# Stacking phi beside P in the attention stage of an attention + two-MoE kernel

## The chip, the cores and the metric

The kernel runs on one core of a Trainium2 chip. The metric is the device time of one execution in microseconds, taken over several runs; a profile of one execution gives the trace.

## The reference

Three layers follow each other. The first is attention with a memory, for B = 4 batches, H = 8 heads, S = 576 tokens and D = 64; its output, transposed to 2304 tokens of 512 numbers, goes through two feed-forward layers of 512 -> 2048 -> 512 with weights in 64 bits, the first with mish, the second with silu.

```python
scores = scale * q @ k.T                       # causal, then softmax
local  = softmax(scores) @ v
phi    = lambda x: np.where(x > 0, x, np.exp(x) - 1) + 1
mem    = (phi(q) @ M_prev) / (phi(q) @ z_prev + 1e-6)
g      = sigmoid(beta)
attn   = g * mem + (1 - g) * local
h = attn @ w_in;  out1 = (h * tanh(softplus(h))) @ w_out     # layer 1
h = out1 @ w_in2; out  = silu(h) @ w_out2                    # layer 2
```

phi(q) is also exp(min(q, 0)) + max(q, 0).

## The kernel before

The attention stage works on 16 pairs of heads (two heads of one batch at a time, head 0 in partitions 0 to 63 and head 1 in 64 to 127 where that matters). Every step of a pair is a named operation: `pair_steps` gives its engine, an assumed duration and what it needs, `Attn.steps` what it issues. A planner (`Steps.plan`) lists all operations of the program in order of a latest time plus an offset for its kind (`SHIFT`), and that order is the order in which each engine's queue runs; nothing at run time waits for the planner's times. Engines: P = TensorE, D = VectorE (DVE), A = ScalarE (ACT), G = GpSimd (POOL), S = the DMA queue of SyncE.

For each pair:

- Loads: `ldkT`, `ldqT`, `ldnq` (q by tokens), `ldnv`.
- Scores: TensorE makes q k for query blocks 4, 3, 2, 1 (128 queries each) and 0 (64 queries) in PSUM ring `s` (L561, L597); DVE adds the mask and takes the row minimum in one pass (`r..`, L554); ACT takes the exponential into tiles P4 to P0 and sums rows into `z` (`e..`, L578).
- phi: `phe` = exp(q) and `phu` = q + 1 on ACT (L502, L503), `phf` = max(min(e, 1), u) on DVE (L504), `phz` = phi times z_prev on POOL (L506), `phr` the row sum on DVE (L508), `phg`, `phd` small DVE steps (L509, L512), `phq` multiplies by the row sums (L513), `phm` scales phi by that on POOL (L515). Each of them works on 640 columns, of which a half of the first 128 is zero padding.
- Row sums: `za` on DVE (L604) and `zd`, the reciprocal (L606); POOL makes `zg` (the factors, L607) and `n00` (block 0 scaled, L610).
- Transpositions: TensorE turns P, phi (`T`), the factors (`RT`) and block 0 (`Xs`) by 64x64 blocks into PSUM ring `t` (L483). The copies out of PSUM go to `W0` (phi under or over P's first 64 keys) and to `h1`, `h2`, `h3` (the other keys), by ACT (`hi`, L473) and DVE (`vec`, L476). phi and P's first keys come from different transpositions, so each copy into `W0` fills 64 partitions.
- Values: `Vhi`, `Vlo` multiply with v and M_prev on TensorE (L667); `Vhic`, `Vloc` (DVE, L671) and `Vlo0` (ACT) write the result to `xT`.

Beside this the weights of the first MoE group are decoded from 64 bits during attention: eight jobs, each with four DVE steps (L787, L789, L791, L794), and some steps of them on POOL (L820, L839). After attention, `open0` and `open1` hand PSUM and SBUF to the MoE part; its products (L973 to L975) and second matmuls (L1041) fill TensorE until the end.

Of the kernel before, what the change touches and what calls it, by code (L numbers as in the profile page):

```python
# [202 lines left out]
P = 128  # L203
B, H, S, D = 4, 8, 576, 64
# [19 lines left out]
def dve(n):  # L224
# [7 lines left out]
}  # L232
AB = "AB"
# [23 lines left out]
def pair_steps():  # L257
# [4 lines left out]
    E("phe", "A", act(640, False), ["ldnq"])  # L262
    E("phu", "A", act(640, False), ["ldnq"])
    E("phf", "D", dve(640), ["phe", "phu"])
    E("phz", "G", 1.57, ["phf"])
    E("phr", "D", dve(640), ["phz"])
    E("phg", "D", 0.09, ["phr"])
    E("phd", "D", 0.13, ["phg"], 0.1)
    qk = ["ldkT", "ldqT"]
    for i in (4, 3, 2, 1):  # L270
# [17 lines left out]
        if i == 1:  # L288
            m.group("s", ("s0", "P", 0.25, qk), [("r00", "D", dve(ST), ["s0"], 0.17)])
            E("e00", "A", act(ST, False, 2), ["r00"])  # L290
            m.uses.append(("sm", "r00", ["r00"], ["e00"]))
            exps = ["e00"] + [f"e{x}{y}" for x in range(1, 5) for y in range(2)]
            E("za", "D", 0.15, exps)
            E("zd", "D", 0.15, ["za"], 0.1)
            E("zg", "G", 1.2, ["zd"])
# [37 lines left out]
class Attn:  # L333
# [12 lines left out]
        "W0": ([P, 2, S], F32, ["T", "X1", "X3", "Xs"], VA, 2),
        "P4": ([P, 2, S], F32, ["e40", "e41"], ["X1", "X2"], 2),
        "P3": ([P, 2, width(3)], F32, ["e30", "e31"], ["X1", "X2"], 2),
        "P2": ([P, 2, width(2)], F32, ["e20", "e21"], ["X3"], 2),
        "P1": ([P, 2, width(1)], F32, ["e10", "e11"], ["X3"], 2),  # L350
        "P0": ([P, 2, ST], F32, ["e00"], ["Xs"], 2),
# [5 lines left out]
    TILES["z"] = ([P, 10], F32, ["e00", "e10", "e11", "e20", "e21", "e30", "e31", "e40", "e41"], ["zd", "phq"], 2)  # L357
    TILES["r"] = ([P, 10], F32, ["zd"], ["zg", "n00"], 2)
    TILES["rx"] = ([P, 4, 2, D], F32, ["zg"], ["RT"], 2)
    TILES["R"] = ([P, S - ST], F32, ["RT"], ["Vhic", "Vloc"], 2)  # L360
    for _g in GROUPS:
        TILES[f"h{_g}"] = ([P, 8 if _g == 2 else 6, P], F32, [f"X{_g}"], ["Vlo" if _g == 3 else "Vhi"], 2)
# [20 lines left out]
    def get(self, p, nm):  # L383
        s = self.st[p]
        if nm not in s:
            shape, dt, _, _, cap = self.TILES[nm]
            if nm == "nq":
                s[nm] = self.kept[nm][p % 2]
            else:
                s[nm] = self.pool(nm).tile(shape, dt, tag=nm, name=nm, bufs=cap)  # L390
# [10 lines left out]
    def consts(self):  # L401
        nc, cp, ep = self.nc, self.wp["late"], self.wp["early"]
        self.kept = {"nq": []}
# [17 lines left out]
        for nm, w in (("bt0", H), ("g", H), ("g1", H), ("g1s", NP), ("bt5", 5 * H)):  # L421
            setattr(self, nm, cp.tile([P, w], F32, name=nm))
        for n in range(2):
            t = self.pool("nq").tile([P, 5, 2, D], F32, name=f"nq{n}")
            nc.gpsimd.memset(t[:ST, 0], 0.0)
            self.kept["nq"].append(t)
        self.load(0, "kT", nc.scalar)

    def gates(self):
# [9 lines left out]
        def sig():  # L439
# [4 lines left out]
            b5 = self.bt5.rearrange("p (c h) -> p c h", c=5)  # L444
            for j in range(2):
# [3 lines left out]
            nc.vector.tensor_copy(b5[:, 0, :], bt)  # L449
            nc.vector.tensor_tensor(  # L450
                b5[:, 1:, :], self.g1.unsqueeze(1).to_broadcast([P, 4, H]), bt.unsqueeze(1).to_broadcast([P, 4, H]), op=ALU.mult)
        return ld, exp, sig

    def load(self, p, nm, queue=None):
# [4 lines left out]
        if nm == "nq":  # L459
            queue.dma_start(t[:, 1:].rearrange("p c j d -> p (c j d)"), src[:, 2 * D:])  # L460
            queue.dma_start(t[ST:, 0].rearrange("p j d -> p (j d)"), src[ST:, :2 * D])
        else:
            queue.dma_start(t.rearrange("p c j d -> p (c j d)") if nm == "nv" else t, src)
        bt = self.bt[b]
        if hp == 0 and nm == "nq":
# [3 lines left out]
                self.z[b].rearrange("h d -> (h d)").unsqueeze(0).to_broadcast([P, H * D]))  # L469

# [14 lines left out]
    def kcols(self, j, w):  # L485
        return slice(S + ST - w, S + ST) if j else slice(0, w)

    def mcols(self, j, w):
        return self.mask[:, S - P:S - P + w] if j else self.mask[:, S - w:S]

    def steps(self, p):
# [6 lines left out]
        for nm in ("kT", "qT", "nq", "nv"):  # L498
# [14 lines left out]
        f["phq"] = lambda: nc.vector.tensor_tensor(  # L513
            s["c"][:, 1:], s["c"][:, 1:], s["z"][:, 2:].rearrange("p (c j) -> p c j", j=2), op=ALU.mult)
        f["phm"] = lambda: nc.gpsimd.tensor_tensor(  # L515
            s["e"], s["e"], s["c"].unsqueeze(3).to_broadcast([P, 5, 2, D]), op=ALU.mult)

        def T():
            s["TA"], s["TB"] = self.psum("t"), self.psum("t")
            e = s["e"].rearrange("p c j d -> p c (j d)")  # L520
            self.halves((s["TA"], s["TB"]), [(e[R[0], c] if c else None, e[R[1], c]) for c in range(5)])
        f["T"] = T

        def Th(a):
            for j in range(2):
                w = G("W0")[R[j], j, :]
                ps = s["T" + a].rearrange("p (c x) -> p c x", x=ST)[R[j]]
                if a == "A":
                    self.hi(w[:, ST:].rearrange("p (c x) -> p c x", x=P)[:, :, :ST], ps[:, 1:5])
                else:  # L530
                    self.hi(w.rearrange("p (c x) -> p c x", x=ST)[:, ::2], ps[:, :5])
# [68 lines left out]
        def r00():  # L600
# [4 lines left out]
            s["z"][:, 1:], s["z"][:, 1:], 1.0, 1e-9, op0=ALU.mult, op1=ALU.add)  # L605
        f["zd"] = lambda: nc.vector.reciprocal(G("r")[:, 1:], s["z"][:, 1:])  # L606
        f["zg"] = lambda: nc.gpsimd.tensor_tensor(  # L607
            G("rx"), s["r"][:, 2:].rearrange("p (c j) -> p c j", j=2).unsqueeze(3).to_broadcast([P, 4, 2, D]),
            self.g1[:, h0:h0 + 2].unsqueeze(1).unsqueeze(3).to_broadcast([P, 4, 2, D]), op=ALU.mult)
        f["n00"] = lambda: nc.gpsimd.tensor_scalar(  # L610
            s["P0"], s["P0"][:, 1].unsqueeze(1).to_broadcast([P, 2, ST]), s["r"][:, 1:2],
            self.g1s[:, hp:hp + 1], op0=ALU.mult, op1=ALU.mult)

        def X(g):
# [3 lines left out]
            for key, chunks in GROUPS[g]:  # L618
# [801 lines left out]
```

## Time and profile before

| | us |
|---|---|
| median of 3 runs (lowest, highest) | 989.54 (987.35, 991.29) |
| the profiled execution, its time | 987.81 |
| its span, first to last instruction | 985.2 |
| mean granted TensorE clock, share of full | 0.994 |
| busy: TensorE 938.0, DVE 698.3, ACT 532.0, POOL 94.1 | |

The profile's rows are of the profiled execution; its time is 2.6 us above its span, and 1.73 us below the median. The page cuts the span into 40 slices of 24.6 us; attention fills the first nine.

### The profile page before, as it was taken

What the parts mean: (1) busy time and instruction counts of PE and PEld (TensorE: products, weight loads), DVE (VectorE), ACT (ScalarE), POOL (GpSimd) and SP (SyncE); (2) the same over time, 40 slices, a digit from 0 to 9 for tenths busy, and PEclk for the clock granted to TensorE, in tenths of its full rate; (3) what the DMA queues carried; (4) which work ended last, traced back from release to release, by engine and by line L of the source; (5) the groups of instructions that cost most, each with busy time, mean ns of one, the idle gap of its engine ahead of it and who ended that gap; (6) DMA issues with size and microseconds to landing.
All of it is one profiled execution on the core that took longest, in us unless ns stands there. A gap on an engine that the chain in (4) does not pass through costs nothing.

```text
span 985.2 us, 17546 instructions
## 1 busy us (share of the span) xinstructions
PE 938.0 (95%) x6672; PEld 823.0 (84%) x6672; DVE 698.3 (71%) x1635; ACT 532.0 (54%) x1263; POOL 94.1 (10%) x97
## 2 busy tenths in 40 slices
PE   5888888889999999999999999999999999999998
PEld 3555555568999999989999998898898988898986
DVE  6899999999569665774767699947654955564333
ACT  6899999878555424343343465745443433434330
POOL 3346454430000000000000000000000000000000
PEclk9899999999999999999999999999999999999999
DMA  6444444146646640364055453741570356024412
GB/s 209 120 124 135 124 134 124 50 154 249 248 144 178 234 161 1 116 226 165 24 191 212 186 234 119 261 129 44 195 249 22 94 192 208 15 72 160 149 54 96
DMA packets 56323, 142.95 MB, mean 145 GB/s; under 512 B 5040, under 2 KB 23472, under 8 KB 56240
## 3 DMA queue, kind: packets, MB, share of 16 engines
q1 hardware_dynamic: 56096, 141.52, 42.3%
q8 instruction: 52, 0.85, 0.4%
q10 hardware_dynamic: 144, 0.33, 0.1%
q14 instruction: 31, 0.25, 0.1%
HBM read 104.08 MB, written 37.75 MB: 144 GB/s over the span
## 4 chain that ended last, share of the span: by engine, by line
PE 80%; DVE 11%; ACT 6%; issue 2%; DMA 1%; POOL 0%; SPq 0%; DVEq 0%; POOLq 0%; ACTq 0%
PE acc L1041 41%; PE psX L973 7%; PE psX L974 7%; PE psX L975 7%; PE psY L974 3%; PE psY L973 3%; PE psY L975 3%; DVE sm L554 3%; ACT P L578 3%; PE ps_s L561 2%; PE psW L973 2%; PE psW L974 2%; PE psW L975 2%; DVE h L476 1%; ACT W L473 1%
## 5 line engine op out<-in xcount | busy, mean ns | idle before, releaser
L1041 PE MATMUL acc<-g,w 128*128 128x320 f32 (+1 forms) x1152 | 218.1, 337 | 0.0
L1041 PE MATMUL acc<-w,g 128*128 128x512 f32 x864 | 216.5, 394 | 0.0
L1041 PEld LDWEIGHTS acc<-g,w 128*128 128x128 f32 x1152 | 183.9, 188 | 13.2
L1041 PEld LDWEIGHTS acc<-w,g 128*128 128x128 f32 x864 | 157.1, 188 | 29.4
L1004 ACT COPY vt<-psX 128x256 f32<-128x256 f32 (+1 forms) x192 | 75.9, 398 | 181.3 <-PE psX L975 177.6
L1062 DVE TENSOR_TENSOR xT<-acc,xT 128x512 f32<-128x512 f32 (+1 forms) x126 | 77.1, 613 | 78.1 <-PE acc L1041 77.1
L1014 DVE TENSOR_TENSOR g<-vt,g 128x640 fp32r<-128x640 f32 (+1 forms) x128 | 94.5, 753 | 43.8 <-ACT g L1013 43.3
L1002 DVE TENSOR_TENSOR vt<-psY,vt 128x256 f32<-128x256 f32 (+1 forms) x128 | 57.6, 455 | 78.2 <-PE psY L975 45.8
L1013 ACT CAST g<-vt 128x640 fp32r<-128x640 f32 (+1 forms) x128 | 83.0, 672 | 29.7 <-PE acc L1041 28.6
L578 ACT ACTIVATE P<-sm,m 128x448 f32<-128x448 f32 (+4 forms) x144 | 83.2, 579 | 6.9 <-DVE m L554 6.3
L561 PE MATMUL ps_s<-kT,qT 64*128 64x288 f32 (+3 forms) x320 | 70.3, 479 | 9.6 <-DMA qT<-in_qT_dram 7.9
L973 PE MATMUL psX<-x,w 128*128 128x256 f32 (+1 forms) x256 | 75.7, 296 | 0.0
L974 PE MATMUL psX<-x,w 128*128 128x256 f32 (+1 forms) x256 | 75.6, 295 | 0.0
L975 PE MATMUL psX<-x,w 128*128 128x256 f32 (+1 forms) x256 | 75.6, 295 | 0.0
L1002 DVE TENSOR_TENSOR vt<-psW,vt 128x256 f32<-128x256 f32 (+1 forms) x64 | 29.1, 455 | 50.9 <-PE psW L975 50.8
L1010 ACT ACTIVATE vt<-vt 128x640 f32<-128x640 f32 (+1 forms) x64 | 43.7, 685 | 39.4 <-DVE vt L1002 39.4
L483 PEld LDWEIGHTS ps_t<-ident,P 64*128 64x128 f32 x800 | 35.3, 140 | 34.4 <-DVE xT L671 11.3
L483 PE MATMUL ps_t<-ident,P 64*128 64x64 f32 x800 | 45.4, 231 | 15.9 <-DVE xT L671 6.8
L1008 ACT ACTIVATE vt<-vt 128x256 f32<-128x256 f32 (+1 forms) x64 | 28.5, 446 | 56.3 <-DVE vt L1002 56.2
L554 DVE CUSTOM_DVE_ANT_0 sm<-ps_s,mask 128x288 f32<-128x288 f32 (+3 forms) x128 | 57.1, 467 | 1.2 <-ACT P L578 0.7
L1009 ACT ACTIVATE vt<-psX 128x256 f32<-128x256 f32 (+1 forms) x64 | 26.1, 409 | 49.7 <-PE psX L975 49.4
L973 PEld LDWEIGHTS psX<-x,w 128*128 128x128 f32 x256 | 48.2, 188 | 2.5 <-issue 0.2
(114 smaller groups left out, 2020.2 us busy)
## 6 DMA issues: line engine op xcount, KB each, us to landing
stg<-in_moe_w_in_dram SPq DMA_DIRECT2D x32, 512.0 KB, 5.5
stg<-in_moe_w_out_dram SPq DMA_DIRECT2D x32, 512.0 KB, 4.1
x<-sp SPq DMA_DIRECT2D x18, 640.0 KB, 5.5
x<-sp SPq DMA_DIRECT2D x18, 512.0 KB, 4.7
sp<-x SPq DMA_DIRECT2D x12, 640.0 KB, 3.7
sp<-x SPq DMA_DIRECT2D x12, 512.0 KB, 3.9
nv<-in_v_dram SPq DMA_DIRECT2D x16, 320.0 KB, 3.5
x1T<-sp01T SPq DMA_DIRECT2D x8, 640.0 KB, 5.0
```

The lines of the kernel that those rows point to most:

```text
L483: self.nc.tensor.transpose(to[:, n * ST:(n + 1) * ST], src[x], self.ident[r, r])
L554: nc.vector.tensor_tensor_reduce(out, ps, mask, -0.125, init, ALU.add, ALU.min, acc)
L561: nc.tensor.matmul(ps, lhsT=s["qT"][R[j], qcols(i)], rhs=s["kT"][R[j], k0 + cols.start:k0 + cols.stop], start=True, stop=True)
L578: nc.scalar.activation(G(f"P{i}")[:, 1 - j if i else 1], s[f"sm{i}{j}"], AF.Exp, bias=s[f"m{i}"][:, j:j + 1], scale=-1.0, accum_out=G("z") ...
L973: nc.tensor.matmul(o, lhsT=W(0, kc), rhs=X(0, kc), start=(n in (1, 2, 7) and kc == 0), stop=False, skip_group_check=True)
L974: nc.tensor.matmul(o, lhsT=W(0, kc), rhs=X(1, kc), start=False, stop=False, skip_group_check=True)
L975: nc.tensor.matmul(o, lhsT=W(1, kc), rhs=X(0, kc), start=False, stop=(kc == 1), skip_group_check=True)
L1002: nc.vector.tensor_tensor(o, self.bank[q, to], o, op=ALU.add)
L1013: f[f"h{c}"] = lambda c=c: nc.scalar.copy(hi(c), val(c))
L1014: f[f"l{c}"] = lambda c=c: nc.vector.tensor_tensor(self.gt(q, c)[:, 1, :2 * tb], val(c), hi(c).bitcast(F32), op=ALU.subtract)
L1041: nc.tensor.matmul(y, lhsT=a, rhs=b, start=(c == 0 and k == 0), stop=(c == 1 and k == 5))
L1062: nc.vector.tensor_tensor(part, acc, part, op=ALU.add)
```

## The change

phi no longer has its own transposition. For query blocks 1 to 4, P is written as `[P of head 0 | phi of both heads | P of head 1]` in one row (tiles `Ph` for blocks 3 and 4, `Pl` for 1 and 2; keys of one head now run backwards so that its first 64 keys lie next to phi). A 128-column slice then holds P's first 64 keys and phi side by side, and one transposition (`W`, 16 of them) stacks both over 128 partitions. Block 0 does the same inside `X3`. So `T`, `Xs` and the copies of 64 partitions are gone: each copy out of PSUM has 128 partitions. The copies are shared out by the list `ON_ACT`; the others are on DVE.

phi is exp(min(q, 0)) + max(q, 0) over 576 columns (no padding): `phn` and `phu` (min, max), `phf` (the sum), `phz` and `phy` (times z_prev) on POOL, `phe` (the exponential) alone on ACT. `phm` becomes `phmh`, `phml`, `phm0` on POOL, which write into the P tiles. One DMA loads q instead of two; z_prev gets two more small loads for each batch. The factors' tile `rx` moves to the pool that `open0` waits for, and so `open0` now waits for `zg` and `RT` instead of `T`. The whole `SHIFT` table has new values; `PERIOD` stays.

```diff
-    E("phe", "A", act(640, False), ["ldnq"])
-    E("phu", "A", act(640, False), ["ldnq"])
-    E("phf", "D", dve(640), ["phe", "phu"])
-    E("phz", "G", 1.57, ["phf"])
-    E("phr", "D", dve(640), ["phz"])
+    E("phn", "G", 0.75, ["ldnq"])
+    E("phe", "A", 0.58, ["phn"])
+    E("phu", "G", 0.75, ["ldnq"])
+    E("phf", "G", 1.25, ["phe", "phu"])
+    E("phz", "G", 1.25, ["phf"])
+    E("phy", "G", 0.36, ["phf"])
+    E("phr", "D", dve(576), ["phz", "phy"])
...
+ON_ACT = ("WA", "X1A", "X2A", "X2B", "X3A")
...
+    def evict(n, d, deps, w, more=0.0):
+        m.twin("t", (n, "P", d, deps), [
+            [(f"{n}{a}h", "A", act(w) + more, [n]) if n + a in ON_ACT else (f"{n}{a}h", "D", dve(w) + more, [n])] for a in AB])
...
-            E("phm", "G", 1.28, ["phq"])
+            E("phmh", "G", 0.75, ["phq"])
+            E("phml", "G", 0.75, ["phq"])
+            E("phm0", "G", 0.36, ["phd"])
...
-            m.twin("t", ("T", "P", 0.45, ["phm"]), [[("TAh", "A", 0.58, ["T"])], [("TBh", "A", 0.69, ["T"])]])
+            evict("W", 0.52, ["phmh", "phml"] + exps[1:], 512)
...
-            for g in (1, 2):
-                X(g, hi)
+            evict("X1", 0.52, hi, 512)
+            evict("X2", 0.42, hi, 384)
...
-            X(3, lo)
-            m.twin("t", ("Xs", "P", 0.12, ["n00"]), [[("XsAh", "D", 0.23, ["Xs"])], [("XsBh", "D", 0.23, ["Xs"])]])
+            evict("X3", 0.48, lo + ["n00", "phm0"], 384, 0.14)
...
-        f["phe"] = lambda: nc.scalar.activation(self.get(p, "e"), s["nq"], AF.Exp)
-        f["phu"] = lambda: nc.scalar.activation(self.get(p, "u"), s["nq"], AF.Identity, bias=1.0)
-        f["phf"] = lambda: nc.vector.scalar_tensor_tensor(
-            out=s["e"], in0=s["e"], scalar=1.0, in1=s["u"], op0=ALU.min, op1=ALU.max)
+        f["phn"] = lambda: nc.gpsimd.tensor_scalar(self.get(p, "e"), s["nq"], 0.0, None, op0=ALU.min)
+        f["phe"] = lambda: nc.scalar.activation(s["e"], s["e"], AF.Exp)
+        f["phu"] = lambda: nc.gpsimd.tensor_scalar(self.get(p, "u"), s["nq"], 0.0, None, op0=ALU.max)
+        f["phf"] = lambda: nc.gpsimd.tensor_tensor(s["e"], s["e"], s["u"], op=ALU.add)
...
+        f["phy"] = lambda: nc.gpsimd.tensor_tensor(s["u"][:, 8], s["e"][:, 8], self.bt[b]["y"][:, hp], op=ALU.mult)
...
+        def Wh(a):
+            x = AB.index(a)
+            put("W", a)(G("W0")[:, :, ST:].rearrange("p j (c x) -> p j c x", x=P)[:, :, :, x * ST:(x + 1) * ST],
+                        s["W"][x].rearrange("p (j c x) -> p j c x", j=2, x=ST))
...
+            bt["y"] = self.wp["early"].tile([P, NP, D], F32, tag="y", name="y", bufs=2)
+            for j in range(2):
+                queue.dma_start(
...
-        early = [n for n in self.pair.ops if n[:2] in ("ld", "ph") or n[0] in "Tsre"]
+        early = [n for n in self.pair.ops if n[:2] in ("ld", "ph", "zg", "RT") and n[-1] != "h" or n[:2] == "ph" or n[0] in "sre"]
```

## Rows read from the trace of the kernel before

**Rows 1.** The page, the span in 40 slices (busy tenths of each).
```profile
PE   5888888889999999999999999999999999999998
DVE  6899999999569665774767699947654955564333
```

**Rows 2.** Stretches, us: busy PE, PEld, DVE, ACT, POOL (counts), clock, DMA share, GB/s.
```profile
19.94:204.32 184.38, 155.31 (x1751) 103.28 (x1753) 176.07 (x613) 171.59 (x516) 82.55 (x77) 0.97 0.38 115
...
204.32:228.00 23.68, 20.06 (x209) 16.60 (x205) 21.51 (x45) 18.97 (x44) 5.72 (x5) 1.00 0.53 201
228.00:985.00 757.00, 751.88 (x4630) 695.68 (x4628) 488.79 (x932) 329.24 (x673) 0.00 (x0) 1.00 0.43 149
```

**Rows 3.** Lines za, phq, n00: ns min/median/max, first and last start.
```profile
L604 DVE TENSOR_SCALAR z<-z x16: 156/168/1519, 19.9 to 204.3; 128x9 f32<-128x9 f32 x16
...
L513 DVE TENSOR_TENSOR c<-c,z x16: 154/414/1500, 20.4 to 205.0; 128x8 f32<-128x8 f32 x16
...
L610 POOL TENSOR_SCALAR P<-P,r,g1s x16: 447/451/1004, 23.5 to 207.0; 128x128 f32<-128x128 f32 x16
```

**Rows 4.** Busy time of L604 and of L513 alone, stretch 19.94 to 204.32.
```profile
19.94:204.32 184.38, 10.02 (x16) 0.97 0.38 115
...
19.94:204.32 184.38, 10.45 (x15) 0.97 0.38 115
```

**Rows 5.** Timeline near 131 us: start, us, engine, line [idle before, releaser].
```profile
131.26 1.56 POOL L506 TENSOR_TENSOR u<-e,z 128x640 f32<-128x640 f32 x1 [7.30 <-DVE e L504]
...
131.37 1.48 DVE L604 TENSOR_SCALAR z<-z 128x9 f32<-128x9 f32 x1
```

**Rows 6.** Busy time of L476 (DVE copies), then L473 (ACT copies), 19.94 to 204.32.
```profile
19.94:204.32 184.38, 45.55 (x129) 0.97 0.38 115
...
19.94:204.32 184.38, 68.60 (x203) 0.97 0.38 115
```

**Rows 7.** DVE groups by shape, 0 to 200 us: busy us, mean ns | idle before.
```profile
L476 DVE COPY h<-ps_t 128x384 f32<-128x384 f32 x29 | 15.6, 539 | 0.0
...
L504 DVE SCALAR_TENSOR_TENSOR e<-e,u 128x640 f32<-128x640 f32 x16 | 13.2, 822 | 8.4 <-ACT u L503 5.6 <-ACT e L502 2.5
L508 DVE TENSOR_REDUCE c<-u 128x10 f32<-128x640 f32 x15 | 12.1, 807 | 0.0
...
L476 DVE COPY h<-ps_t 128x512 f32<-128x512 f32 x15 | 9.8, 652 | 0.0
...
L476 DVE COPY W<-ps_t 64x64 f32<-64x64 f32 x28 | 6.2, 220 | 0.9 <-PE ps_t L483 0.2
```

**Rows 8.** ACT groups by shape, 0 to 200 us, same columns.
```profile
L473 ACT COPY h<-ps_t 128x384 f32<-128x384 f32 x29 | 13.7, 472 | 0.0
...
L502 ACT ACTIVATE e<-nq 128x640 f32<-128x640 f32 x16 | 11.8, 739 | 3.9 <-DMA nq<-in_q_dram 3.7
L503 ACT ACTIVATE u<-nq 128x640 f32<-128x640 f32 x16 | 11.5, 726 | 0.0
...
L473 ACT COPY R<-ps_t 128x256 f32<-128x256 f32 x28 | 10.1, 365 | 0.7 <-PE ps_t L483 0.4
...
L473 ACT COPY h<-ps_t 128x512 f32<-128x512 f32 x15 | 8.6, 571 | 0.1
...
L473 ACT COPY xT<-ps_t 128x64 f32<-128x64 f32 x13 | 2.7, 211 | 2.3 <-DVE xT L671 1.5 <-PE ps_t L667 0.8
```

**Rows 9.** POOL groups by shape, 0 to 200 us, same columns.
```profile
L607 POOL TENSOR_TENSOR rx<-r,g 128x512 f32<-128x512 f32 x15 | 15.6, 1041 | 0.0
...
L839 POOL TENSOR_TENSOR val<-val 128x256 f32<-128x256 f32 x6 | 4.4, 729 | 0.2
...
L820 POOL TENSOR_TENSOR w<-val,w 128x512 fp32r<-128x512 f32 x2 | 2.5, 1272 | 0.0
...
L410 POOL MEMSET mask<- 128x1024 f32 x1 | 1.0, 953 | 0.0
```

**Rows 10.** One DMA issue at the start, SyncE's queue: start, us.
```profile
1.80 0.57 SPq L467 DMA_DIRECT2D z<-in_z_prev_dram  x1
```

More of the change, by code (lines that the diff above doesn't have):

```diff
@@ L338 @@
     TILES = {
-        "nq": ([P, 5, 2, D], F32, ["ldnq"], ["phe", "phu"], 2),
+        "nq": ([P, 9, D], F32, ["ldnq"], ["phn", "phu"], 2),
         "nv": ([P, 5, 2, D], F32, ["ldnv"], VA, 2),
-        "e": ([P, 5, 2, D], F32, ["phe"], ["T"], 2),
-        "u": ([P, 5, 2, D], F32, ["phu"], ["phr"], 2),
-        "c": ([P, 5, 2], F32, ["phr"], ["phm"], 2),
+        "e": ([P, 9, D], F32, ["phn"], ["phmh", "phml", "phm0"], 2),
+        "u": ([P, 9, D], F32, ["phu"], ["phr"], 2),
+        "c": ([P, 9], F32, ["phr"], ["phmh", "phml", "phm0"], 2),
         "qT": ([P, S], F32, ["ldqT"], SC + ["s0"], 3),
         "kT": ([P, S + ST], F32, ["ldkT"], SC + ["s0"], 3),
[L346 to L351, printed above, removed]
+        "W0": ([P, 2, S], F32, ["W", "X3"], VA, 2),
+        "Ph": ([P, 2 * (width(3) + P + width(4))], F32, ["e30", "e31", "e40", "e41"], ["X1", "X2", "W"], 2),
+        "Pl": ([P, 2 * (width(1) + P + width(2))], F32, ["e10", "e11", "e20", "e21"], ["X3", "W"], 2),
+        "P0": ([P, 3, ST], F32, ["e00", "phm0"], ["X3"], 2),
     }
@@ L356 @@
         TILES[f"m{_i}"] = ([P, 4], F32, _r, _e, 2)
-    TILES["z"] = ([P, 10], F32, ["e00", "e10", "e11", "e20", "e21", "e30", "e31", "e40", "e41"], ["zd", "phq"], 2)
-    TILES["r"] = ([P, 10], F32, ["zd"], ["zg", "n00"], 2)
+    TILES["z"] = ([P, 9], F32, ["e00", "e10", "e11", "e20", "e21", "e30", "e31", "e40", "e41"], ["zd", "phq"], 2)
+    TILES["r"] = ([P, 9], F32, ["zd"], ["zg", "n00"], 2)
     TILES["rx"] = ([P, 4, 2, D], F32, ["zg"], ["RT"], 2)
@@ L361 @@
     for _g in GROUPS:
[L362 removed]
+        TILES[f"h{_g}"] = ([P, 8 if _g == 1 else 6, P], F32, [f"X{_g}"], ["Vlo" if _g == 3 else "Vhi"], 2)
     def __init__(self, tc, xT, q, qT, kT, v, z, beta, T=13.5):
@@ L386, in get @@
             shape, dt, _, _, cap = self.TILES[nm]
[L387 to L390, printed above, removed]
+            s[nm] = self.pool(nm).tile(shape, dt, tag=nm, name=nm, bufs=cap)
         return s[nm]
     def pool(self, nm):
-        late = nm in ("W0", "nv", "z", "r", "rx", "R") or nm[0] in "Ph" and nm[1:].isdigit()
+        late = nm in ("W0", "nv", "z", "r", "R") or nm[0] == "P" or nm[0] == "h"
         return self.wp["late" if late else "early"]
@@ L420, in consts @@
                 compare_op=ALU.is_ge, fill=-8.0e9, base=0, channel_multiplier=1)
-        for nm, w in (("bt0", H), ("g", H), ("g1", H), ("g1s", NP), ("bt5", 5 * H)):
+        for nm, w in (("bt0", H), ("g", H), ("g1", H), ("g1s", NP), ("btg", H), ("bt9", NP * 9)):
             setattr(self, nm, cp.tile([P, w], F32, name=nm))
[L423 to L426, printed above, removed]
         self.load(0, "kT", nc.scalar)
@@ L458, in load @@
         t = self.get(p, nm)
[L459 to L463, printed above, removed]
+        to = t.rearrange("p s d -> p (s d)") if nm == "nq" else t.rearrange("p c j d -> p (c j d)") if nm == "nv" else t
+        queue.dma_start(to, src)
         bt = self.bt[b]
@@ L469, in load @@
                 self.z[b].rearrange("h d -> (h d)").unsqueeze(0).to_broadcast([P, H * D]))
+            bt["y"] = self.wp["early"].tile([P, NP, D], F32, tag="y", name="y", bufs=2)
+            for j in range(2):
+                queue.dma_start(
+                    bt["y"][j * ST:(j + 1) * ST],
+                    self.z[b].rearrange("(n j) d -> j n d", j=2)[j].unsqueeze(0).to_broadcast([ST, NP, D]))
     def hi(self, h, src):
@@ L485, in kcols @@
     def kcols(self, j, w):
-        return slice(S + ST - w, S + ST) if j else slice(0, w)
+        return slice(0, w) if j else slice(S + ST - w, S + ST)
     def mcols(self, j, w):
-        return self.mask[:, S - P:S - P + w] if j else self.mask[:, S - w:S]
+        return self.mask[:, S - w:S] if j else self.mask[:, S - P:S - P + w]
     def steps(self, p):
@@ L512, in steps @@
         f["phd"] = lambda: nc.vector.reciprocal(s["c"], s["c"])
[L513 to L521, printed above, removed]
@@ L522, in steps @@
-        f["T"] = T
-        def Th(a):
-            for j in range(2):
[L526 to L531, printed above, removed]
+        f["phq"] = lambda: nc.vector.tensor_tensor(s["c"][:, :8], s["c"][:, :8], s["z"][:, :8], op=ALU.mult)
@@ new lines, in base, with ptile, phm @@
+        def base(i):
+            return 2 * width(i - 1) + P if i in (2, 4) else 0
+        def ptile(i):
+            return G("Ph" if i > 2 else "Pl")
+        def phm(x):
+            i = 3 if x == "h" else 1
+            t = ptile(i)
+            m0 = width(i)
+            o = t.rearrange("p (c k) -> p c k", c=2)[:, :, m0:m0 + P].rearrange("p c (j d) -> p c j d", j=2)
+            a = slice(2 * (i - 1), 2 * (i + 1))
+            nc.gpsimd.tensor_tensor(
+                o, s["e"][:, a].rearrange("p (c j) d -> p c j d", j=2),
+                s["c"][:, a].rearrange("p (c j) -> p c j", j=2).unsqueeze(3).to_broadcast([P, 2, 2, D]), op=ALU.mult)
@@ new lines, in steps, with W @@
+        for x in "hl":
+            f["phm" + x] = lambda x=x: phm(x)
+        f["phm0"] = lambda: nc.gpsimd.tensor_tensor(
+            G("P0")[:, 1], s["e"][:, 8], s["c"][:, 8:9].to_broadcast([P, D]), op=ALU.mult)
+        def W():
+            ps = s["W"] = (self.psum("t"), self.psum("t"))
+            blocks = []
+            for j in range(2):
+                for i in range(1, 5):
+                    o = base(i) + width(i) + (ST if j else -ST)
+                    src = ptile(i)[:, o:o + P]
+                    blocks.append((src[R[0]], src[R[1]]))
+            self.halves(ps, blocks)
@@ L533, in steps, with put @@
+        f["W"] = W
+        def put(n, a):
+            return self.hi if n + a in ON_ACT else self.vec
+        def Wh(a):
+            x = AB.index(a)
+            put("W", a)(G("W0")[:, :, ST:].rearrange("p j (c x) -> p j c x", x=P)[:, :, :, x * ST:(x + 1) * ST],
+                        s["W"][x].rearrange("p (j c x) -> p j c x", j=2, x=ST))
         for a in AB:
-            f[f"T{a}h"] = lambda a=a: Th(a)
+            f[f"W{a}h"] = lambda a=a: Wh(a)
         def RT():
@@ L633, in Xh @@
             x = AB.index(a)
-            ps, to = s[f"X{g}"][x].rearrange("p (n x) -> p n x", x=ST), G(f"h{g}")
-            put = self.vec if x else self.hi
-            if g != 2:
-                q0 = HI0 if g == 1 else ST
-                for j in range(2):
-                    w = G("W0")[R[1 - j], j, q0:q0 + 2 * P].rearrange("p (n x) -> p n x", x=P)
-                    put(w[:, :, x * ST:(x + 1) * ST], ps[R[1 - j], :2])
-                ps = ps[:, 2:]
-            put(to[:, :, x * ST:(x + 1) * ST], ps)
+            n = 8 if g == 1 else 6
+            ps = s[f"X{g}"][x].rearrange("p (n x) -> p n x", x=ST)
+            to = put(f"X{g}", a)
+            to(G(f"h{g}")[:, :, x * ST:(x + 1) * ST], ps[:, :n])
+            if g == 3:
+                to(G("W0")[:, x, :ST], ps[:, n])
         for g in GROUPS:
@@ L1389, in laid_out @@
     m = x["M_prev"].reshape(B, NP, 2, D, D)
-    top = np.stack([m[:, :, 0], first[:, :, :, 1]], axis=3)
-    low = np.stack([first[:, :, :, 0], m[:, :, 1]], axis=3)
+    top = np.stack([first[:, :, :, 0], m[:, :, 1]], axis=3)
+    low = np.stack([m[:, :, 0], first[:, :, :, 1]], axis=3)
     x["v"] = np.concatenate([np.concatenate([top, low], axis=2).reshape(B, NP, P, 2 * D), rest], axis=3)
```

87 lines of the change are left out of this document (41 added, 46 removed), and 169 rows, old and new, of tables (GROUPS, SHIFT).

## The prediction

> **What bounds the kernel now.** I read the slices first: TensorE stands at nine tenths in nearly every slice from the tenth on, but at eight tenths in the first nine, while DVE is at nine tenths there and falls afterwards [rows 1]. So there are two stages with two limits. The stretches give the sizes [rows 2]. From 228 us to the end TensorE works 751.88 of 757.00 us: only 5.1 us are idle there, and nothing in this stage is changed but the order of its instructions. The change is worth what it shortens attention by, as everything behind it moves with it.
>
> Then the attention stage. The step za comes once in each pair; its first and last start, 19.9 and 204.3 us, lie 15 periods apart [rows 3]: one period is 184.38 / 15 = 12.29 us. Divided by 15, the busy times of that stretch [rows 2] are, for one pair: DVE 11.74, ACT 11.44, TensorE 10.35, POOL 5.50. DVE is busy 95.5% of the time, ACT 93%. The reader is to see that both have to be relieved, that TensorE stands only 16% below, and that POOL is half free.
>
> The third view is of single instructions. za has 9 columns and takes 0.16 us, at most 1.52; phq has 8 columns, and its median is 0.41, its longest 1.50 [rows 3]. At 131 us one sees why: POOL begins phz at 131.26 for 1.56 us, za begins at 131.37 and lasts 1.48, to just after phz's end [rows 5]. DVE stood still behind a POOL instruction. In total za and phq take 10.02 and 10.45 us in the stretch [rows 4]; 31 of them at 0.16 would be 5.0, so 15.5 us are waits, 1.03 us in each pair.
>
> **The change part by part, for one pair.** The working goes by busy time, as that is what DVE's period is made of.
>
> *DVE.* Its copies out of PSUM cost 45.55 / 15 = 3.04 us [rows 6]. Afterwards there are four: W and X1 with 512 columns (0.652 each), X3 with 384 (0.539) and its 64 columns for block 0 (0.220) [rows 7]: 2.06, so 0.98 less. phf goes to POOL: 0.82 less. phr reads 576 columns in place of 640, 0.807 x 64 / 640 = 0.08 less [rows 7]. Together 1.88: 11.74 becomes 9.86, and without the 1.03 of waits it is 8.83.
>
> What waits come back is the unknown. No row shows POOL so full. Lower bound: none. Upper bound: za, phq, phg and two weight steps (eight jobs of four steps over 16 pairs) each stand behind a POOL instruction for 1.3 us, as the stalled za did: 6.5 us. I take 1.7: five steps, a POOL busy 0.8 of the time, and on average 0.42 us left of the instruction that runs. I lean to the low end since today's collision is built in: phz begins right after phf on DVE, and za follows on DVE. Afterwards phf is on POOL, and phz no longer begins when DVE has just moved on. DVE is then 8.83 + 1.7 = 10.5 us.
>
> *ACT.* Its copies cost 68.60 / 15 = 4.57 [rows 6]. Afterwards: the two of the factors (0.365), W and X1 (0.571 each), three of 384 (0.472), and two of 64 columns (0.211) [rows 8]: 3.71, so 0.86 less. phu is gone (0.726), and phe is 576 wide in place of 640 (a difference of 128 columns costs 0.571 - 0.472, so 64 cost 0.05) [rows 8]. 11.44 - 1.64 = 9.8 us: no bound any more.
>
> *POOL.* phz, phm, zg and n00 go from two wide passes for phi to eight smaller ones. Two-input passes cost 0.729 for 256 columns and 1.272 for 512, so 0.19 + 2.12 ns a column [rows 9]: phf 576 is 1.41, phz 512 1.27, phy 64 0.33. phmh and phml (256 columns, one operand repeated) lie between half of zg's 1.041 and 0.729 [rows 9]; I take 0.60 each, and 0.27 for phm0. phn and phu are tensor_scalar passes of 576. The only such row, n00, takes 0.451 for 128 columns [rows 3]; with 0.19 fixed that is 2.0 ns a column, 1.36 for 576. A memset of 1024 takes 0.953, and 576 / 1024 of it is 0.54 [rows 9]. I take 0.95, between them, as n00 has two scalars to a column and these have one. With zg 1.04 and n00 0.45 the sum is 7.9, from 7.1 to 8.7. The weights' part stays: 5.50 less today's phz (1.56 [rows 5]), phm (zg's 1.041 x 640 / 512 = 1.30), zg and n00 is 1.15. POOL comes to 9.0 us, between 8.2 and 9.8: hidden behind DVE at 11, but no longer half free.
>
> *TensorE.* A pair has 67 transpositions of 64 columns now (T 9, RT 8, X1 to X3 16 each, Xs 2) and 66 afterwards (W 16, RT 8, 16, 12, 14). Nothing is taken off: 10.3 us. That is the floor of the period, however far the others fall.
>
> *The period.* At today's share of 95.5%, 10.5 us on DVE give 11.0 us. 15 periods gain 15 x 1.29 = 19.4 us.
>
> *Ends.* At the start q's two loads become one, and z_prev's load gets two more of about 0.57 us of issue each [rows 10]; SyncE's queue brings qT after them, so the first scores come up to 0.6 us later, though the new order can turn this round. At the end open0 waits for RT, which needs zg's 1.04 us on POOL [rows 9], in place of T: up to 1 us later. Against it stands about 0.5 us less of DVE work on the last pair. I put the ends at +1.0.
>
> *Sum* against the profiled execution: 987.81 - 19.4 + 1.0 = 969.4. Its time is 1.73 us under the median of the runs (989.54), so 971.1; I say 971.
>
> One page speaks against the change. The Trainium skill, SBUF — State Buffer, "Who interferes with whom", says that a copying or tensor_scalar instruction of DVE in a two-port mode, or one with two SBUF inputs, and a GpSimd instruction that reads SBUF exclude each other, the second one waiting until the first is done. The za behind phz [rows 5] agrees. By that rule moving work from DVE to POOL takes time back from DVE; the fourth case below is what it would do here.
>
> **The rivals.** About 0.5% (4.9 us) is what a measurement of this kernel can tell from no change.
>
> 1. As above, DVE still the limit at about 11 us: 971 (964 to 977). Chance 0.52.
> 2. TensorE's floor. The waits nearly vanish, as no DVE step feeds phz any more, and the period falls to 10.35: 15 x 1.94 = 29.1 less, with the ends 959.7, or 961 beside the median. For it: 8.83 on DVE without waits. Against it: four engines within 15% of each other, each in a fixed order, and TensorE idles 29 us in the stretch today [rows 2]. The lowest, 956, takes in a granted clock of 1.0 in place of 0.97 there [rows 2]. Chance 0.16.
> 3. POOL becomes the limit. If phn and phu cost 1.36 each, it has 9.8 us; it also waits for ACT (phe) and DVE (phq) inside each pair, with the passes of the next pair queued behind, and DVE's two-input steps can hold it up. At 85 to 90% busy the period is 11.6: 10.4 less, with the ends 978.4, or 980. For it: its load nearly doubles. Against it: two pairs of phi buffers let it work ahead. Chance 0.18.
> 4. Slower, by the lock between DVE and POOL. It turns the sign when DVE's waits exceed 3.2 us a pair (8.83 + 3.2 = 12.0, at 95.5% a period of 12.6). With 4 us, five steps at 0.8 each, the period is 13.4: 15 x 1.1 + 1.0 more, 1006, or 1007. For it: the waits of 1.3 us [rows 3, 5]. Against it: phi's passes are shorter afterwards, and the median za did not wait. Chance 0.08.
> 5. The gain is not handed on: the first products wait for something else (weights, or an order in the new offsets that costs 10 to 20 us on TensorE), so 989. Against it: the decode steps lie in the same queues and move with the pairs. Chance 0.06.
>
> **How the numbers follow.** 971 is case 1. Cases 1, 2 and 3 are faster by over 0.5%, save for a little of the third: 0.85; within 0.5% is case 5 and that rest: 0.07; slower is case 4: 0.08. The range goes from the lowest of case 2, 956, to 984, beyond case 3; it leaves out cases 4 and 5 and some tails, 0.19.
>
> **What would show it.** za to za 11.0 us, first to last about 165; the first MoE product some 18 us earlier than now; DVE 95% busy in the stretch, ACT 85 to 90%, TensorE 93%, POOL about 82%. Copies out of PSUM at 128 partitions cost 0.65 and 0.57 for 512 columns. za and phq together wait 0.7 us a pair or less; many DVE steps at about 0.5 us, few at 1.5. From 228 us on the work is what it is now, in time 757 us give or take 3. The prediction is wrong if phn and phu cost 1.3 or more, if POOL is above 90%, if DVE's small steps lengthen past 3 us a pair, or if TensorE idles while DVE idles too, which would be the order and not an engine.

## The result, and the profile after

The changed kernel takes 964.57 us (median of 4 runs, 964.39 to 967.41); the kernel before, run beside it, 989.75. The ratio is 0.9754 [0.9728, 0.9781]: 2.5% faster. The forecast was 971, with a range from 956 to 984.

The profiled execution took 967.41 us, against 987.81 before: 20.4 less, where the sum had 18.4 less. It is the longest of the four runs; between the medians the time fell by 25.2 us, where the forecast had 18.5. The slices of the page come first (busy tenths; the last row is TensorE's granted clock).

```profile
PE   6998989889999999999999999999999999999998
DVE  6898889896577668773858798947656756654333
...
POOL 7989999600000000000000000000000000000000
PEclk9898999999999999999999999999999999999999
```

Beside [rows 1], DVE has lost its row of nines in attention; POOL has them now. TensorE's unbroken nines begin in the tenth slice in both, as attention ends less than one slice earlier. The stretches from the first za to the last, and from 212 us on, give the sizes (busy PE, PEld, DVE, ACT, POOL with counts, clock, DMA share, GB/s):

```profile
19.40:184.70 165.30, 149.54 (x1756) 100.97 (x1753) 147.65 (x525) 138.38 (x430) 151.76 (x165) 0.94 0.40 130
212.00:965.50 753.50, 749.04 (x4614) 693.39 (x4613) 489.40 (x929) 328.14 (x668) 0.00 (x0) 1.00 0.43 150
```

Against [rows 2], 15 periods fell from 184.38 to 165.30 us, from 12.29 to 11.02 each. Before the first za 0.5 us were won, behind the last one 0.1 (780.9 to 780.8). So nearly the whole gain is in the pairs, and it is handed on: the first MoE product starts at 195.28 in place of 212.40, 17.1 earlier, and what follows it is 2.6 us shorter. POOL is the fullest engine now: 151.76 of 165.30 is 92%, and DVE has 89%.

The lines that answer to [rows 3], and POOL's wide passes (ns min/median/max, first and last start):

```profile
L628 DVE TENSOR_SCALAR z<-z x16: 161/318/1402, 19.4 to 184.7; 128x9 f32<-128x9 f32 x16
...
L514 DVE TENSOR_TENSOR c<-c,z x16: 100/166/1189, 20.6 to 185.4; 128x8 f32<-128x8 f32 x16
...
L502 POOL TENSOR_SCALAR e<-nq x16: 1641/1650/1849, 5.5 to 172.5; 128x576 f32<-128x576 f32 x16
...
L504 POOL TENSOR_SCALAR u<-nq x16: 1641/1648/1665, 7.1 to 168.0; 128x576 f32<-128x576 f32 x16
...
L505 POOL TENSOR_TENSOR e<-e,u x16: 1402/1414/1921, 9.7 to 175.3; 128x576 f32<-128x576 f32 x16
```

phn (L502) and phu (L504) take 1.65 us each. The minimum is as long as the median, so this is the work itself and no wait. phf (L505) takes 1.41, as forecast. The median of za (L628) has doubled, that of phq (L514) has fallen to the time of the work.

The collision of [rows 5] is still there. From the timeline (start, duration, both in us):

```profile
19.32 1.27 POOL L506 TENSOR_TENSOR u<-e,z 128x512 f32<-128x512 f32 x1
...
19.42 1.20 DVE L628 TENSOR_SCALAR z<-z 128x9 f32<-128x9 f32 x1
```

za ends 0.03 us behind phz's end. Last, two waits from this stretch (who waited for whom: us in total, times, longest):

```profile
POOL P L533 <- DVE c L513: 4.6, 4, 2.9
...
DVE c L510 <- POOL u L509: 4.2, 5, 1.2
```

The two engines wait for each other: phm0 on POOL (L533) waits for phd on DVE (L513), and phr on DVE (L510) waits for phy on POOL (L509).

### The profile page after: what moved, and what is told of

The parts are those of the page before. It is cut to its first block, busy times and chain, and to the rows that moved or that the text cites. A ratio compares the mean times of both kernels' runs of the same rounds, so it can differ in the third digit from the quotient of the medians.

```text
span 965.5 us, 17322 instructions
## 1 busy us (share of the span) xinstructions
PE 932.6 (97%) x6656; PEld 821.3 (85%) x6656; DVE 673.1 (70%) x1541; ACT 496.3 (51%) x1167; POOL 171.1 (18%) x191
## 4 chain that ended last, share of the span: by engine, by line
PE 82%; POOL 6%; ACT 5%; DVE 4%; issue 1%; DMA 1%; SPq 0%; POOLq 0%; ACTq 0%
PE acc L1053 42%; PE psX L985 7%; PE psX L986 7%; PE psX L987 7%; PE psY L986 3%; PE psY L987 3%; PE psY L985 3%; PE ps_t L679 2%; PE psW L987 2%; PE psW L986 2%; PE psW L985 2%; PE ps_s L582 2%; PE ps_t L483 1%; POOL e L502 1%; ACT Ph L602 1%
## 5 line engine op out<-in xcount | busy, mean ns | idle before, releaser
L1026 DVE TENSOR_TENSOR g<-vt,g 128x512 fp32r<-128x512 f32 (+1 forms) x128 | 94.9, 754 | 40.3 <-ACT g L1025 39.4
L1025 ACT CAST g<-vt 128x512 fp32r<-128x512 f32 (+1 forms) x128 | 83.5, 672 | 36.8 <-PE acc L1053 35.7
L985 PE MATMUL psX<-x,w 128*128 128x320 f32 (+1 forms) x256 | 75.8, 296 | 0.0
L986 PE MATMUL psX<-x,w 128*128 128x320 f32 (+1 forms) x256 | 75.7, 296 | 0.0
L987 PE MATMUL psX<-x,w 128*128 128x320 f32 (+1 forms) x256 | 75.6, 295 | 0.0
L575 DVE CUSTOM_DVE_ANT_0 sm<-ps_s,mask 128x320 f32<-128x320 f32 (+3 forms) x128 | 56.6, 472 | 8.9 <-PE ps_s L582 7.2
L985 PEld LDWEIGHTS psX<-x,w 128*128 128x128 f32 x256 | 48.2, 188 | 1.8 <-issue 0.2
L986 PEld LDWEIGHTS psX<-x,w 128*128 128x128 f32 x256 | 48.3, 189 | 1.6
L602 ACT ACTIVATE Ph<-sm,m 128x576 f32<-128x576 f32 (+1 forms) x64 | 45.7, 720 | 6.1 <-DVE m L575 5.8
L987 PEld LDWEIGHTS psX<-x,w 128*128 128x128 f32 x256 | 48.2, 188 | 0.0
```

Of the source, the lines that this page charges most:

```text
L575: nc.vector.tensor_tensor_reduce(out, ps, mask, -0.125, init, ALU.add, ALU.min, acc)
L602: nc.scalar.activation(ptile(i)[:, o:o + w] if i else G("P0")[:, 2], s[f"sm{i}{j}"], AF.Exp, bias=s[f"m{i}"][:, j:j + 1], scale=-1.0, accu ...
L985: nc.tensor.matmul(o, lhsT=W(0, kc), rhs=X(0, kc), start=(n in (1, 2, 7) and kc == 0), stop=False, skip_group_check=True)
L986: nc.tensor.matmul(o, lhsT=W(0, kc), rhs=X(1, kc), start=False, stop=False, skip_group_check=True)
L987: nc.tensor.matmul(o, lhsT=W(1, kc), rhs=X(0, kc), start=False, stop=(kc == 1), skip_group_check=True)
L1025: f[f"h{c}"] = lambda c=c: nc.scalar.copy(hi(c), val(c))
```

## The experiments

The open question was why a forecast made for a full DVE held, when POOL had become the fullest engine. The first account: POOL's queue, made too long by phn and phu, sets the period. The rivals: DVE still sets it, by its own work or by the lock (a DVE step stands still until the POOL instruction that runs is done); TensorE's floor is near; the order does it. Each time below is a median of four to seven runs, and each ratio is to the kernel before, run beside it. L numbers are those of the changed kernel, except in the rows of an edited kernel.

**The changed kernel again**, as a line to measure from.

> The changed kernel as it is, as the yardstick for the others. In its profile za to za is 11.02 us (15 periods in 165.3 us), POOL is busy 91.8% of that stretch, TensorE 90.5%, DVE 89.3%, ACT 83.7%. All theories: 0.975 of the time before, about 964.6 us.

It took 965.67 us, ratio 0.9769 [0.9751, 0.9786], with a period of 163.0 / 15 = 10.87. The differences below are from this run. Its stretch from the first za to the last:

```profile
19.50:182.50 163.00, 147.37 (x1758) 99.06 (x1754) 146.74 (x526) 138.68 (x430) 151.71 (x165) 0.97 0.41 131
```

**phu, then phn too, taken off POOL.**

```diff
-        f["phu"] = lambda: nc.gpsimd.tensor_scalar(self.get(p, "u"), s["nq"], 0.0, None, op0=ALU.max)
+        f["phu"] = lambda: nc.scalar.activation(self.get(p, "u"), s["nq"], AF.Relu)
```
```diff
-        f["phn"] = lambda: nc.gpsimd.tensor_scalar(self.get(p, "e"), s["nq"], 0.0, None, op0=ALU.min)
+        f["phn"] = lambda: nc.vector.tensor_scalar(self.get(p, "e"), s["nq"], 0.0, None, op0=ALU.min)
```

> phu = max(q, 0) on ACT (Relu) in place of POOL, everything else and the order of instructions as in the changed kernel. Theory A (POOL's queue is the limit, as its two 1.65 us passes fill it): POOL loses 1.65 of 10.1 us a pair, the period falls from 11.0 to about 10.5, which the next engines allow (TensorE 10.0, DVE 9.8, ACT 9.2 + 0.6), and the time by 6 to 9 us, to about 957. Theory B (DVE is the limit and waits behind POOL, as predicted): only one POOL instruction of eleven is gone, DVE's waits of about 1 us a pair fall by 0.15, the time by 2 to 3 us, to 962. Theory C (TensorE is the limit, at its lower clock for part of the stage): no change, 964 give or take 1.5.

> phu on ACT (Relu) and phn = min(q, 0) on DVE, order of instructions as in the changed kernel. Theory A: POOL is at 6.8 us a pair and no limit any more, the period comes to rest on TensorE (10.0) at about 10.3 to 10.5, the time at 954 to 957, little below the run with phu alone. Theory B: DVE gets a pass of about 0.4 us more and loses about 0.3 us of waits: no change or 2 us slower than the changed kernel, 964 to 967. Theory C: no change, 964.

With phu on ACT: 961.78 us, 0.9727 [0.9710, 0.9745], 3.9 less. With phn on DVE as well: 956.88, 0.9680 [0.9661, 0.9697], 8.8 less. The stretch between the first and last za, of the one and of the other:

```profile
19.40:179.90 160.50, 146.96 (x1758) 98.77 (x1755) 143.97 (x526) 145.33 (x444) 129.96 (x152) 0.97 0.41 133
```
```profile
19.60:175.10 155.50, 145.57 (x1758) 99.04 (x1755) 145.68 (x539) 145.09 (x444) 108.02 (x137) 0.97 0.43 137
```

POOL falls to 81% and then to 69%. Each 1.65 us taken off it brings 0.25 and 0.3 us a pair, not 1.65: the work went to ACT and DVE, and in the second kernel TensorE, DVE and ACT stand at 93 to 94%. The first time, 961.8, is the 962 of the account with DVE and not the 957 of the account with POOL; the second fits the account with POOL alone. So POOL's load does cost time, but it doesn't set the period by itself.

**One more pass of that kind on POOL**, into a tile that nobody reads.

```diff
+            t = self.wp["early"].tile([P, 9, D], F32, tag="spare", name="spare", bufs=1)
+            nc.gpsimd.tensor_scalar(t, s["nq"], 0.0, None, op0=ALU.max)
```

> The changed kernel with one more POOL pass for each pair (max(q, 0) a second time, into a tile that nobody reads, 1.65 us). Theory A: POOL has 11.8 us for a pair, the period rises to about 12 or more, the time by 13 to 25 us, to 978 to 990. Theory B: DVE's waits rise by about 0.15 us a pair, the time by 2 to 3 us. Theory C: no change.

985.29 us, 0.9966 [0.9953, 0.9978]: 19.6 more for 16 x 1.65 = 26.4 us of work, or 0.74 of it. The period is 12.12, and POOL is busy 95.8%:

```profile
20.20:202.00 181.80, 155.47 (x1756) 104.18 (x1753) 150.00 (x525) 139.77 (x430) 174.16 (x179) 0.90 0.37 118
```

DVE's wait for phy's result grows from 4.2 us in the changed kernel's profile to 10.6. TensorE's granted clock is 0.90 in this stretch, and 0.97 in the kernel measured from; with TensorE busy 86% of the time this can be a part of the price, which is not taken apart. The lock could also do this, as the pass keeps DVE out. But a DVE step that stands still counts as busy, as za's 1.20 us did, and DVE's busy time grew only from 146.74 / 15 = 9.78 to 150.00 / 15 = 10.00 us a pair, where the period grew by 1.25. The last experiment of this list asks the same in another way.

**One more pass on DVE**, a second row sum into a tile that nobody reads.

```diff
+            t = self.wp["early"].tile([P, 9], F32, tag="spare", name="spare", bufs=1)
+            nc.vector.tensor_reduce(out=t, in_=s["u"], axis=AX.X, op=ALU.add)
```

> The changed kernel with one more DVE pass for each pair (phr's row sum a second time into a tile that nobody reads, 0.75 us; it has one SBUF input). Theory A: DVE goes from 9.8 to 10.5 of a period of 10.9, so POOL's limit hides most of it: 0 to 5 us slower, 965 to 970. Theory B: 15 x 0.75 / 0.95 = 12 us slower, 977. The POOL pass of 1.65 us cost 19.6.

973.34 us, 0.9846 [0.9832, 0.9861]: 7.7 more for 16 x 0.74 = 11.8 us, or 0.65 of it. The time lies in neither range, above the 970 of the account with POOL and below the 977 of that with DVE. A microsecond on DVE, at 89%, costs nearly as much as one on POOL, at 92%. So neither of the two sets the period alone; the chain goes through both, as the two waits above show. The pass stands inside phi's chain, between phr and phg, and whether DVE's load or the longer chain is what costs isn't told apart here.

**phi back on its old engines**, the stacking and the copies kept, the order kept: exp(q) and q + 1 on ACT, max(min(e, 1), u) on DVE.

```diff
-        f["phn"] = lambda: nc.gpsimd.tensor_scalar(self.get(p, "e"), s["nq"], 0.0, None, op0=ALU.min)
-        f["phe"] = lambda: nc.scalar.activation(s["e"], s["e"], AF.Exp)
-        f["phu"] = lambda: nc.gpsimd.tensor_scalar(self.get(p, "u"), s["nq"], 0.0, None, op0=ALU.max)
-        f["phf"] = lambda: nc.gpsimd.tensor_tensor(s["e"], s["e"], s["u"], op=ALU.add)
+        f["phn"] = None
+        f["phe"] = lambda: nc.scalar.activation(self.get(p, "e"), s["nq"], AF.Exp)
+        f["phu"] = lambda: nc.scalar.activation(self.get(p, "u"), s["nq"], AF.Identity, bias=1.0)
+        f["phf"] = lambda: nc.vector.scalar_tensor_tensor(
+            out=s["e"], in0=s["e"], scalar=1.0, in1=s["u"], op0=ALU.min, op1=ALU.max)
```

> The changed kernel with phi's passes where they were before: exp(q) and q + 1 on ACT, max(min(e, 1), q + 1) on DVE, phn dropped; 576 columns, stacked transpositions and full-height copies stay, and so does the order. POOL loses phn, phu and phf (4.7 of 10.1 us a pair), ACT gains 0.68 (9.25 to 9.9), DVE gains 0.75 (9.8 to 10.5, less what it no longer waits for POOL). Theory A (POOL is the limit of the changed kernel, so phi's move gave nothing by itself): about the changed kernel's time or faster, 955 to 966. Theory B (DVE is the limit): DVE 10.6 over 0.95 gives a period of 11.1 in place of 10.9, 967 to 970.

956.79 us, 0.9680 [0.9666, 0.9695]: 8.9 less than the changed kernel. Its stretch, then its za from the lines:

```profile
20.50:173.50 153.00, 144.20 (x1758) 97.94 (x1754) 143.45 (x540) 144.97 (x444) 86.79 (x123) 1.00 0.43 139
```
```profile
L629 DVE TENSOR_SCALAR z<-z x16: 161/170/578, 20.5 to 173.5; 128x9 f32<-128x9 f32 x16
```

The period is 10.2, with TensorE, DVE and ACT at 94 to 95% and POOL at 57%. The waits of za, phq and phg together fall to 0.24 us a pair. So the move of phi to POOL is no part of the gain; it takes 9 us away from it.

**phi on POOL alone**, in the kernel before: the same four passes (640 columns), its transpositions, copies and order as they were.

> The kernel before, with phi's passes on POOL as in the change (min, max and the sum; exp on ACT) but nothing stacked: 640 columns, the old transpositions and copies, the old order. POOL goes from 5.5 to about 10.7 us a pair, DVE loses phf (0.82 of 11.74), ACT loses 0.73 of 11.44. Theory A (POOL's load and DVE's waits behind it take back what phi's move frees): 983 to 998. Theory B (DVE's own work sets the period): 15 x 0.82 / 0.955 = 13 us faster, 976.

1003.85 us, 1.0139 [1.0111, 1.0167]: slower by 14 us, and beyond the 998 that was the most either account gave. The period is 13.03; the stretch, then za from the lines:

```profile
23.50:219.00 195.50, 161.56 (x1751) 106.70 (x1753) 173.59 (x598) 163.59 (x503) 150.51 (x117) 0.93 0.35 108
```
```profile
L606 DVE TENSOR_SCALAR z<-z x16: 157/888/1255, 23.5 to 219.0; 128x9 f32<-128x9 f32 x16
```

POOL is at 77% here, and za's median is 0.89 us. One reservation: the old order puts phe and phu side by side on ACT, so POOL's phf waits 17.1 us for the exponential; a new order might take part of the 14 us back.

**The full height of the copies**: W's copies made in two halves of 64 partitions each.

```diff
-            put("W", a)(G("W0")[:, :, ST:].rearrange("p j (c x) -> p j c x", x=P)[:, :, :, x * ST:(x + 1) * ST],
+            for r in R:
+                put("W", a)(G("W0")[r, :, ST:].rearrange("p j (c x) -> p j c x", x=P)[:, :, :, x * ST:(x + 1) * ST],
```

> The changed kernel with each of the two copies of W split into two of 64 partitions and 512 columns: 0.57 us more on ACT and 0.65 on DVE for each pair. Theory A: POOL's limit covers most of it, DVE goes from 9.8 to 10.4 and ACT from 9.25 to 9.8 of a period of 10.9; 0 to 5 us slower, 965 to 970. Theory B: 15 x 0.65 / 0.95 = 10 us slower, 975.

973.23 us, 0.9849 [0.9832, 0.9865]: 7.6 more, again between the two ranges. A copy of 512 columns costs the same for half the partitions (DVE, both rows from the lines of the two kernels by form, the halved one second):

```profile
L476 DVE COPY W<-ps_t 128x512 f32<-128x512 f32 x15 | 10.3, 686 | 0.3 <-PE ps_t L483 0.2
```
```profile
L476 DVE COPY W<-ps_t 64x512 f32<-64x512 f32 x30 | 20.6, 685 | 0.2
```

That is 0.69 us a pair more on DVE and 0.58 on ACT.

**The order of before**: only the values of `SHIFT` are those of the kernel before (as far as the names still exist).

> The changed kernel with the offset table of the kernel before (steps that it does not know get no offset), so only the order of the instructions differs. If the order is worth little in either stage: 964 to 970. If the new offsets carry part of the gain (the first loads in another order, POOL's queue in another order): 972 to 985, seen as a longer period of za or more idle TensorE after attention.

975.67 us, 0.9863 [0.9842, 0.9884]: 10.0 more. The first za starts at 22.9 in place of 19.5 (3.4 us), and the period is 11.3 in place of 10.87 (15 x 0.43 = 6.5). Beside the 2.3% of the whole change, about 1% hangs on the order.

**An order for the faster version.** Once the planner knows that phe and phu are on ACT and phf on DVE, and once more with a shorter period as well.

```diff
-    E("phn", "G", 0.75, ["ldnq"])
-    E("phe", "A", 0.58, ["phn"])
-    E("phu", "G", 0.75, ["ldnq"])
-    E("phf", "G", 1.25, ["phe", "phu"])
+    E("phe", "A", 0.60, ["ldnq"])
+    E("phu", "A", 0.60, ["ldnq"])
+    E("phf", "D", dve(576), ["phe", "phu"])
```
```diff
-PERIOD = 10.582
+PERIOD = 10.0
```

> Stacked transpositions and full-height copies with phi on ACT and DVE as in the run with phi on the old engines (956.8), but the planner is told so: phe and phu on ACT with 0.60 us, phf on DVE with 0.67, no phn; the offsets stay. Only the order differs from that run. If its order, which was made for another split, costs something: 948 to 956. If the offsets fit only the plan for which they were found: 957 to 970.

> As the run before, with the planner's PERIOD at 10.0 in place of 10.582, nearer to the 10.2 us that the run with phi on the old engines had for a pair: 946 to 960, or 960 to 975 if the offsets fit only the old plan.

966.05 us, 0.9752 [0.9724, 0.9780], and 964.61, 0.9741 [0.9714, 0.9769]: 8 to 9 us above 956.79 with the same instructions, or 6 to 7 by the ratios, as the kernel before took 1.5 us more beside them. The hope that a better-informed planner gives a better order failed: the offsets fit the plan for which they were found, and with other durations they give another order. What offsets made for this version would give stays open.

**The spare POOL pass where POOL is not full**: the same added instruction as above, in the version with phi on its old engines.

> Phi on the old engines with everything stacked (956.8), plus the same spare POOL pass of 1.65 us for each pair that cost the changed kernel 19.6 us. POOL is busy 57% of the stage there and 73% with it, so its queue is no limit in either. If POOL's price is its queue alone: 0 to 2 us slower, 957 to 959. If it is paid through DVE's steps, which wait for the POOL instruction that runs: DVE's small steps wait 0.24 us a pair there and would wait 0.3 to 0.6 us more, 4 to 10 us slower, 961 to 967.

957.60 us, 0.9683 [0.9670, 0.9697]: 0.8 more, which is within the noise, for the same work that cost 19.6 in the changed kernel. Its stretch, then the added pass from the lines:

```profile
21.10:176.10 155.00, 145.35 (x1756) 98.48 (x1753) 145.32 (x540) 145.33 (x444) 109.67 (x137) 0.99 0.42 138
```
```profile
L507 POOL TENSOR_SCALAR spare<-nq x16: 1642/1647/1843, 5.4 to 158.9; 128x576 f32<-128x576 f32 x16
```

POOL goes from 57 to 71%, and the waits of za, phq and phg from 0.24 to 0.31 us a pair. DVE is fuller here (94%) than in the changed kernel (89%), so a lock on its steps would be expected to cost more here, not less. POOL's idle time takes the pass in: it falls from 153.00 - 86.79 = 66.2 us to 45.3, while the changed kernel has 11.3 us of it and the added pass leaves 7.6. The price of a POOL pass comes from how full POOL's queue is, and not from the lock on DVE's steps. What stays open is how much the place in the queue adds: in the changed kernel the pass also stands before phf, which is on POOL there.

## Why the prediction held, and where its steps did not

**The place and the size.** The limit of the kernel was attention's period, and what follows moved with it, as said: 15 periods gave 19.1 us (forecast 19.4), and from the first MoE product to the end it is 770.2 us in place of 772.8, with TensorE idle for 4.5 us from 212 on, about what it was [rows 2]. That fit is of the longest run, though: in the profile of the repeated kernel, near the median, 15 periods gave 184.38 - 163.0 = 21.4. The ends, put at +1.0, gave 0.6 back: the first scores start at 4.70 us, not later than the 7.87 of before, so the new order of the loads outweighs the two added issues.

**The step that failed** is *POOL*: "9.0 us, between 8.2 and 9.8: hidden behind DVE at 11". It measured 151.76 / 15 = 10.12, above its upper bound, and was hidden behind nothing. The term is phn and phu, taken at 0.95 each with 1.36 as the top: they take 1.65. The top had come from n00's row by taking off a fixed 0.19 us that belongs to two-input passes, and the value taken leaned on the memset, which reads nothing. n00 and the new rows together give (1.650 - 0.451) / 448 = 2.7 ns a column, if the two kinds of pass cost the same for a column. The prediction had named both signs that it would be wrong by, 1.3 for a pass and POOL above 90%, and both came. The mechanism is that of its third rival, with a price of 980.

**Why the number held anyway.** By luck: other terms were too high, and the errors cancel. ACT came to 9.23 against 9.8 (its copies 3.19, not 3.71), DVE's copies to 1.96 against 2.06. The forecast had added mean durations there and taken them from busy time; in the trace ACT's copies overlap, their durations add up to 3.66 us a pair, and busy time counts an overlap once. DVE's waits were taken at 1.7 a pair. za, phq and phg show 8.47 + 7.02 + 6.86 in the stretch, less 45 x 0.16 of work, or 1.0 a pair; za and phq alone 0.71, where 0.7 was named. Together DVE has 9.84 against 10.5, and without those 1.0 it has 8.84, the 8.83 of the sum. The period was 10.5 / 0.955 = 11.0 in the forecast, and is 10.12 / 0.918 = 11.02 in the trace: a shorter DVE behind a longer POOL. It is also not the 11.6 of the third rival, as POOL ran at 92% where that put 85 to 90.

**TensorE's floor** of 10.3 us a pair was wrong as well. The transpositions fell from 3.85 us a pair to 3.44 here and 3.28 with phi on its old engines, with nearly the same count (955 and 962 in 15 periods), and TensorE's sum to 9.97 and 9.61. That made 956.8 possible, at the very bottom of the range. The prediction counted transpositions, but their busy time also depends on how many separate bursts they come in. In the changed kernel's timeline 16 in one burst take 0.71 us, and a lone one 0.22:

```profile
102.36 0.71 PE L483 MATMUL ps_t<-ident,Ph 64*128 64x64 f32 x16
...
103.45 0.22 PE L483 MATMUL ps_t<-ident,Pl 64*128 64x64 f32 x1
```

Each further one in a burst adds 0.49 / 15 = 0.03 us, so a burst less saves an estimated 0.19 us. Counted in the trace, the transpositions of 15 periods come in 119 unbroken bursts before and in 82 in both later kernels: 37 x 0.19 / 15 = 0.47 us a pair, where 0.40 was measured. The short bursts of T and Xs are gone, and fewer long ones are broken by a wait. The granted clock fell from 0.97 to 0.94 there, so it is not what shortened them; the further 0.16 us, at the same 82 bursts, goes with a clock of 1.00. No run here changes the number of bursts alone.

**The fourth rival**, slower by the lock, was right in its mechanism and wrong in its weight. By the Trainium skill, SBUF — State Buffer, "Who interferes with whom", a tensor_scalar of DVE in a two-port mode and a GpSimd instruction exclude each other. The trace agrees for one instruction (za lasts 1.20 us behind phz's 1.27, and 0.16 at its shortest), but 26.4 us more of such POOL work cost 0.8 us of time where POOL was at 57%. What makes the time is how full POOL's queue is.

**What the parts are worth.** Four kernels make a table of two by two, as ratios to the kernel before:

| | phi on ACT and DVE | phi on POOL |
|---|---|---|
| old transpositions and copies | 1 | 1.0139 |
| stacked, full height | 0.9680 | 0.9754 (again: 0.9769) |

Stacking with copies of full height gives 3.2%, some 32 us, together with the new order (10 us in the changed kernel), the single load of q and phi's 576 columns in place of 640, which are not taken apart; moving phi to POOL costs 9 us of it. The two kernels at 956.8 beat the changed kernel; the simpler one, phi on its old engines with 576 columns, is the best version found here.

## What to carry to other kernels

Work moved to a half-free engine is priced by how full that engine becomes: the same 1.65 us pass cost 0.03 of its work, no more than noise, with POOL at 57%, and 0.74 with POOL at 92%. Before moving it, bound the operation's duration by rows of the same kind on that engine, with all of the row's time and no fixed part borrowed from another kind; and if the engine would be the fullest at the upper bound, take that as the forecast's case. When a change has two halves, run each alone: a gain of 2.5% hid a half worth 3.2% and a half that cost nearly 1%.

## What the runs showed of the hardware

A pass of POOL with one input and one constant over 576 columns takes 1.65 us (2.9 ns a column), more than its addition of two tiles of the same width, 1.41. The same minimum takes 0.46 on DVE, in the kernel that has phn there (its line):

```profile
L502 DVE TENSOR_SCALAR e<-nq x16: 443/458/1160, 5.4 to 163.4; 128x576 f32<-128x576 f32 x16
```

Halving the partitions of a copy of 512 columns out of PSUM saves nothing, 685 ns against 686. A lone 64x64 transposition shows as 0.22 us of busy TensorE, and 16 in one burst as 0.71. And the spare POOL pass costs 19.6 / 16 = 1.23 us a pair in the changed kernel, but 0.8 / 16 = 0.05 where POOL is half free.
